# A fused attention, top-1 expert and tanh-MLP kernel: one-hot marks of twelve tiles and expert 0's weighing on ScalarE, float64 loads and conversions re-timed

## The chip, the cores and the metric

The kernel runs on one core of one Trainium2 chip. The metric is the device time of one execution, in microseconds (us); lower is better. Three runs of the kernel before took 1000.67, 1001.55 and 1002.6 us, median 1001.55 us. The program uses TensorE (PE, its weight load shown apart as PEld), VectorE (DVE), ScalarE (ACT), GpSimd (POOL) and the DMA queues, most of them issued by SyncE (SP).

## What is computed

Three stages follow each other. The reference, cut to what matters:

```python
# 1. linear attention, B, H, S, D = 4, 8, 768, 64
for t in range(S):
    state = gamma[None, :, None, None] * state + einsum('bhd,bhe->bhde', k[:, :, t], v[:, :, t])
    y[:, :, t] = scale * einsum('bhd,bhde->bhe', q[:, :, t], state)
# 2. top-1 mixture of experts, 3072 tokens, 512 features, 8 experts, 1024 hidden
logits = x @ w_gate;  e_idx = argmax(logits, axis=1);  gate_w = softmax(logits)[e_idx]
eom = sigmoid(x @ w_output_gate)
out[mask] = gate_w[mask, None] * eom[mask, e, None] * (maximum(x[mask] @ w1[e], 0) @ w2[e])
# 3. MLP, hidden 2048
h = x @ w_in;  out = (h - tanh(h)) @ w_out
```

The weights of the MLP come as float64 and everything else as float32. A float32 product is done as three matmuls of a high and a low part.

## The kernel before

**Tiles and stages.** The tokens are 24 tiles of 128 (`NT`, four sequences of six chunks). Stage one is the loop over `n` from 0 to 22 (with the tail behind it, L908 to L1075): in turn `n`, `attend(n)` computes the attention of tile n, `scores(n + 2)` the score matrix of the tile two ahead, and `rows(n)` turns tile n into token rows, stores them to `xtok` and gets the gate logits `lp`. Stage two runs the experts in steps of 128 hidden features (`mm1`, `mm2`), the largest-first order being found at run time; expert 0 is split into a head of 216 tokens (`PLACES[0]`) and a rest. Stage three runs 6 blocks of 512 tokens through 16 hidden slices (`mm3`, `act`, `mm4`).

**What sets the order.** Every engine works its own instructions in the order in which the program wrote them. The loop over n writes them by hand: operations of VectorE that may be late are kept in lists (`scales` for the gating, `convs` for the conversions) from which `fill` takes some at the end of each turn, up to `MOST` (2.6); those of ScalarE are taken by `pump`. SP works its DMAs in program order as well, and a DMA that waits holds all behind it.

**Turn n on TensorE** is: the state's part of the output (`qd`, `st`, L672), the state update (`up`, L680), the outputs (`o`, L690), the scores of tile n + 2 (`sc`, L631), and the transposes with the gate logits in their last columns (`tr`, L716). ScalarE copies the state (`st`, L684), then the outputs (`xT`, L699), which `tr` reads, then the rows (`xr`, L719), and issues their store. VectorE masks the scores (`pt`, L624) and sums the logits (`lp`, L723). GpSimd scales q and k (`qd`, `kd`).

**Gating.** The tiles are gated in groups of 8, 7 and 9 (`GROUPS`); the last group in three cuts. For a group: `onehot` finds each token's expert, `ranks` its rank among that expert's tokens, `scale` the gate value, and a **mark** per tile (L799) writes a 128 x 432 one-hot row of the rank, `ohr = (iota == rank)`. `slots` (`ip`, L859) multiplies the marks with the values into a table of slots. Behind group 1, `head` takes expert 0's first 216 slots from it and starts two gathers of token rows (`gx`); two turns later `weigh` multiplies them with the gate values (L391) and `half` transposes them (`xt`, L406), for `mm1(0)`.

**Conversions.** Each float64 piece (`m64`, two buffers) is loaded by `load_m` (L263) and converted by ten operations of `conv_m`: ScalarE takes the upper word (`keep`, L277), five VectorE operations build the float32 (L280, L283, L289, L293, L298), ScalarE rounds it to the high part (`keep` again, L305), VectorE subtracts (L310). L293 is the last reader of `m64`. Both parts are then stored (`dh`, `dl`, L312, L313). Five pieces are converted in stage one (numbers 27 to 31, pool `cva`, with two buffers each of `keep`, `ta` and `va`), the other 27 in stage two (pool `cv`, `keep` 3, `ta` 2, `va` 2); of these the last three are stored as well.

```python
if n > 0 and nload < NPA and len(m64) < 2 and n >= 2 * nload + 1:
    load_m(J0 + nload, cva_p)
...
if nconv < nload and n >= loaded_at[nconv] + 3:
    convs.append(piece(J0 + nconv, cva_p))
...
fill([scales, *convs], MOST - busy)
```

At n = 19 (`EARLIER`) the loop runs whatever is left of the conversions, since their pool is given to the experts.

Of the kernel before, what the change touches and what calls it, by code (L numbers as in the profile page):

```python
# [8 lines left out]
F32 = mybir.dt.float32  # L9
# [6 lines left out]
AF = mybir.ActivationFunctionType  # L16
ALU = mybir.AluOpType
# [6 lines left out]
P = 128  # L24
# [25 lines left out]
NV = 5 * E  # L50
GROUPS = (8, 7, 9)
TA = sum(GROUPS[:2])
MOST = 2.6
FAR = 1.0e6
PG = P + 2 * E
NPA = 5
# [77 lines left out]
def kernel(  # L134
# [30 lines left out]
    tri = cpool.tile([P, P], BF16, name="tri")  # L165
    ones = cpool.tile([P, P], BF16, name="ones")
    nc.vector.memset(ones, 1.0)
    rank = cpool.tile([P, NT], F32, name="rank")
    emax = cpool.tile([P, NT], F32, name="emax")
    gates = cpool.tile([P, NT], F32, name="gates")  # L170
# [85 lines left out]
            ops.pop(0)[1]()  # L256
            most -= 1

    m64, mcv, cv_bufs = {}, {}, {}

    def load_m(j, cv_p):
        t = cv_p.tile([P, DM], I64, tag="m64", name=f"m64_{j}", bufs=2)
# [3 lines left out]
    def conv_m(j, stage, cv_p):  # L266

        V = nc.vector
        f, cs = j // 2, slice((j % 2) * DM, (j % 2 + 1) * DM)

        def word(w):
            return m64[j].bitcast(U32).rearrange("p (n w) -> p n w", w=2)[:, :, w]

        def begin():
            t = {k: cv_p.tile([P, DM], U32, tag=k, name=f"{k}{j}", bufs=b) for k, b in cv_bufs[cv_p].items()}
            mcv[j] = t
            nc.scalar.activation(f32(t["keep"]), f32(word(1)), AF.Copy, scale=DOWN)  # L277

        def v0():
            V.tensor_scalar(mcv[j]["ta"], mcv[j]["keep"], 4, 1, op0=ALU.logical_shift_left, op1=ALU.logical_shift_right)  # L280

        def v1():
            V.scalar_tensor_tensor(  # L283
                out=mcv[j]["va"], in0=mcv[j]["keep"], scalar=0x80000000, in1=mcv[j]["ta"],
                op0=ALU.bitwise_and, op1=ALU.bitwise_or,
            )

        def v2():
            V.tensor_scalar(mcv[j]["ta"], mcv[j]["va"], 0xFF800000, None, op0=ALU.bitwise_and)  # L289

        def v3():
            sc = f32(mcv[j]["ta"])
            V.scalar_tensor_tensor(out=sc, in0=word(0), scalar=2.0 ** -52, in1=sc, op0=ALU.mult, op1=ALU.mult)  # L293
            m64.pop(j)

        def v4():
            vf = f32(mcv[j]["va"])
            V.tensor_tensor(out=vf, in0=vf, in1=f32(mcv[j]["ta"]), op=ALU.add)  # L298

        def high():  # L300
            if f < NRES:
                mcv[j]["hl"] = [x[:, cs] for x in wres[f]]
            else:
                mcv[j]["hl"] = [mcv[j][k].bitcast(F32R) for k in ("keep", "ta")]
            nc.scalar.activation(mcv[j]["hl"][0], f32(mcv[j]["va"]), AF.Copy)  # L305

        def rest():
            t = mcv.pop(j)
            hi, lo = t["hl"]
            V.tensor_tensor(out=lo, in0=f32(t["va"]), in1=f32(hi), op=ALU.subtract)  # L310
            if f >= NRES:
                stores.append(lambda: nc.sync.dma_start(wdram[f][0][:, cs], f32(hi)))  # L312
                stores.append(lambda: nc.sync.dma_start(wdram[f][1][:, cs], f32(lo)))  # L313

        return [
            [("A", begin)],
            [("V", v0), ("V", v1), ("V", v2)],
            [("V", v3), ("V", v4)],
            [("A", high)],
            [("V", rest)],  # L320
        ][stage]
# [64 lines left out]
    def weigh(p, c):  # L386
        rs = chunk(p, c)
        t = gxs[p, c][rs]
        rank_, c0, _ = PLACES[p]
        if p == 0:  # L390
            nc.vector.tensor_scalar(t, t, head_s[:, c:c + 1], None, op0=ALU.mult)  # L391
        elif p == 1:
            nc.vector.tensor_scalar(t, t, first_s[:, c0 + c, 0:1], None, op0=ALU.mult)
        else:
            nc.scalar.activation(t, t, AF.Copy, scale=sslot[rs, rank_, c:c + 1])
# [163 lines left out]
    with ExitStack() as actx:  # L559
# [221 lines left out]
            lg = t["lg"] if lg is None else lg  # L781
            nc.vector.tensor_tensor(out=t["z"], in0=t["oh"], in1=lg[:, :, E:2 * E], op=ALU.mult)

        def ranks(gi, n0, g0, g1, later=None):
            t = {k: v[:, g0:g1] for k, v in gst[gi].items() if k != "part"}
            G = g1 - g0
            oh = t["oh"]
            pre = bank("pt", f"pre{gi}_{g0}")[:, 0:G * E].rearrange("p (g e) -> p g e", e=E)
            nc.tensor.matmul(pre, ones, cnt.unsqueeze(1).to_broadcast([P, G, E]), start=True, stop=False)
            for g in range(G - 1):  # L790
                nc.tensor.matmul(
                    pre[:, g + 1:G], ones, oh[:, g].unsqueeze(1).to_broadcast([P, G - 1 - g, E]), start=False, stop=False
                )
            nc.tensor.matmul(pre, tri, oh, start=False, stop=True)
            nc.vector.tensor_tensor(out=t["rt"], in0=oh, in1=pre, op=ALU.mult)
            nc.vector.reduce_sum(out=rank[:, n0 + g0:n0 + g1], in_=t["rt"], axis=AX.X)
            for g in range(G):
                def mark(g=g):
                    nc.vector.tensor_scalar(  # L799
                        t["ohr"][:, g], iota, rank[:, n0 + g0 + g:n0 + g0 + g + 1], None, op0=ALU.is_equal  # L800
                    )

                if later is None:
                    mark()
                else:
                    later.append(("V", mark, 0.35))
            if G > 1:
                add = gp.tile([P, E], F32, tag="add", name=f"add{gi}_{g0}")
                nc.vector.reduce_sum(out=add, in_=oh.rearrange("p g e -> p e g"), axis=AX.X)
            else:  # L810
                add = oh[:, 0]
            nc.vector.tensor_tensor(out=cnt, in0=cnt, in1=add, op=ALU.add)
# [101 lines left out]
        nld = 4  # L914
        decay(2)
        J0 = 2 * NFM - NPA
        convs, scales, after = [], [], []
        due, now = {}, [0]
        nload, nconv, busy = 0, 0, 0.0
        loaded_at = []  # L920
        firsts = [sum(GROUPS[:i]) for i in range(len(GROUPS))]
        for n in range(NT - 1):
# [8 lines left out]
                flush()  # L931
                rooms()

            if n > 0 and nload < NPA and len(m64) < 2 and n >= 2 * nload + 1:
                load_m(J0 + nload, cva_p)
                loaded_at.append(n)
                nload += 1
# [3 lines left out]
            if n == TA or nld == NT:  # L941
                feed()
            flush()
            if nconv < nload and n >= loaded_at[nconv] + 3:
                convs.append(piece(J0 + nconv, cva_p))
                nconv += 1
            if n == 6:
                nc.gpsimd.tensor_copy(iota, ca[:, C_IOTA:C_IOTA + NS])
            if n > 0:
                attend(n)  # L950
            if n + 3 < NCH:
                decay(n + 3)
            pump(scales, False)
            for ops in convs:
                pump(ops, False)
# [7 lines left out]
                mm1(0)  # L963
            if n > 0:
                rows(n, gst[gi]["lp"][:, g])
            ready, after = after + due.pop(n, []), []
            for fn in ready:
                fn()

            q = n - (NT - 7)  # L970
            if 0 <= q < 3:
                conv_w(q, 0)
            if 1 <= q < 4:
                conv_w(q - 1, 1)
            if n == NT - 2:
                conv_w(3, 0)
                conv_w(3, 1)
            cuts = [0, G - 3, G - 1] if final else [0, G]
            if g + 1 in cuts[1:]:
                g0 = cuts[cuts.index(g + 1) - 1]  # L980
# [5 lines left out]
                if final and g + 1 == G - 1:  # L986
                    tail_a = a
                else:
                    hi = 2 * E if final else NV

                    def settle(a=a, hi=hi):
                        slots(a[0], a[2], a[3], 0, hi)
                        if a[0] == 1:
                            head()
                            for k in range(2):
                                due.setdefault(now[0] + 2, []).append(lambda k=k: weigh(0, k))
                            for kk in range(KD):
                                due.setdefault(now[0] + 2, []).append(lambda kk=kk: half(kk))

                    def place(a=a, hi=hi, settle=settle):  # L1000
                        ranks(*a, scales)
                        if a[0] == 1:
                            due.setdefault(now[0] + 1, []).append(close)
                        scales.append(("V", lambda: after.append(settle)))

                    after.append(place)
                    if not final:
                        scales += scale(gi, n0, g0, g + 1)
            fill([scales, *convs], MOST - busy)
            busy = 0.0  # L1010
            now[0] = n + 1
        run(scales)
        flush()
        gi, n0, G = len(GROUPS) - 1, firsts[-1], GROUPS[-1]
        for m in sorted(due):
            for fn in due[m]:
                fn()
        attend(NT - 1)
        if 0 not in hs:
            mm1(0)  # L1020
# [98 lines left out]
    for i in range(NFE, NSTEP + 1):  # L1119
# [25 lines left out]
        if i == CONV - 2:  # L1145
            whl2_p.release()
            cv_p = tc.alloc_tile_pool(name="cv", bufs=1, side="right", reuse_waits="tile")
            cv_bufs[cv_p] = dict(keep=3, ta=2, va=2)
            load_m(0, cv_p)
            load_m(1, cv_p)  # L1150
        for op in slot[1]:
# [307 lines left out]
```

## Time and profile before

| what | value |
|---|---|
| median of three runs | 1001.55 us (1000.67 to 1002.6) |
| the profiled execution: its own time | 1006.25 us |
| its span (first to last instruction) | 1004.5 us |
| PE busy | 971.4 us (97%) |
| PEld busy | 841.9 us (84%) |
| DVE busy | 759.4 us (76%) |
| ACT busy | 602.5 us (60%) |
| POOL busy | 375.1 us (37%) |
| mean granted TensorE clock | 0.981 of full speed |

All times below are counted from the start of the span. An engine's busy share is an average over the stages: stage one ends at about 146 us, where the rest of expert 0 begins, the experts at about 459 us, the MLP at the end. A wait in the views is named by the tile that waits, the line that wrote the instruction, and the tile or transfer that released it; where the engine named had long been done, a transfer released it.

### The profile page before, as it was taken

To read this page: it belongs to the slowest core of one execution; us is meant where nothing else is said; L and a number is where in the kernel's file an instruction comes from. 1 tells how busy PE (TensorE), PEld (TensorE's weight loads), DVE (VectorE), ACT (ScalarE), POOL (GpSimd) and SP (SyncE) were. 2 spreads that over 40 slices of the span, in tenths; PEclk is the share of its full clock that TensorE was granted. 3 is DMA by queue.
4 is the path that set the end of the run, shared out by engine and by line. 5 is a ranking of instruction groups with operands and counts; after the bars stand their busy time and mean duration, and the time that the engine had idled before them with its cause. 6 is when DMAs were issued, how large, how long until landed. Compare 5 with 4: busy or idle time off the path is not lost. (4 is left out here: it accounts for less than half of the span.)

```text
span 1004.5 us, 16476 instructions
## 1 busy us (share of the span) xinstructions
PE 971.4 (97%) x5942; PEld 841.9 (84%) x5942; DVE 759.4 (76%) x1189; ACT 602.5 (60%) x1090; POOL 375.1 (37%) x327
## 2 busy tenths in 40 slices
PE   8889889999999999999999999999999999999995
PEld 6778779999999999998888888888888888888884
DVE  2688667788889899866977777777777777777772
ACT  3434333655556565646866776766676767677662
POOL 4553512344354344232432433252343325323322
PEclk9999789999999999999999999999999999999998
DMA  9989624577577677666000100010010001000001
GB/s 333 343 348 368 217 85 146 158 230 218 179 233 221 187 238 222 190 213 219 22 11 11 42 21 22 11 53 11 12 42 22 22 1 54 10 1 21 22 1 45
DMA packets 43579, 120.70 MB, mean 120 GB/s; under 512 B 9334, under 2 KB 14710, under 8 KB 40546
## 3 DMA queue, kind: packets, MB, share of 16 engines
q1 hardware_dynamic: 34450, 99.31, 30.2%
q0 software_dynamic: 4864, 12.91, 4.2%
q10 hardware_dynamic: 4176, 7.36, 2.0%
q8 instruction: 48, 0.79, 0.3%
q14 instruction: 41, 0.34, 0.1%
HBM read 95.99 MB, written 23.57 MB: 119 GB/s over the span
## 5 line engine op out<-in xcount | busy, mean ns | idle before, releaser
L1207 POOL TENSOR_TENSOR gl<-g,gh 128x512 fp32r<-128x512 f32 x96 | 124.0, 1292 | 343.4 <-ACT gh L1206 328.3
L241 POOL TENSOR_TENSOR wl<-wr,wh 128x512 fp32r<-128x512 f32 x64 | 90.2, 1409 | 179.8 <-ACT wh L239 176.2
L1200 DVE COPY_PREDICATED g<-big,td 128x512 f32<-128x512 int32 x96 | 145.2, 1513 | 9.9
L1225 PE MATMUL mh<-x2h,ml 128*128 128x512 f32 x384 | 152.7, 398 | 0.0
L1225 PE MATMUL mh<-x2l,mh 128*128 128x512 f32 x384 | 152.4, 397 | 0.0
L1225 PE MATMUL mh<-x2h,mh 128*128 128x512 f32 x384 | 151.9, 396 | 0.0
L1239 PE MATMUL ma<-ml,gh 128*128 128x512 f32 x384 | 151.3, 394 | 0.0
L1239 PE MATMUL ma<-mh,gh 128*128 128x512 f32 x384 | 151.1, 393 | 0.0
L1239 PE MATMUL ma<-mh,gl 128*128 128x512 f32 x384 | 149.3, 389 | 0.0
L1190 DVE SCALAR_TENSOR_TENSOR g<-s,mh 128x512 f32<-128x512 f32 x96 | 65.9, 686 | 102.1 <-ACT s L1188 86.1
L1186 ACT ACTIVATE u<-mh 128x512 f32<-128x512 f32 x96 | 57.4, 598 | 128.8 <-PE mh L1225 124.7
L239 ACT ACTIVATE wh<-wr 128x512 fp32r<-128x512 f32 x136 | 83.5, 626 | 81.6 <-PE ya L453 75.5
L429 PE MATMUL ph<-xh,wh 128*128 128x216 f32 (+7 forms) x288 | 98.2, 341 | 0.0
L453 PE MATMUL ya<-lo,wh 128*128 128x216 f32 (+7 forms) x288 | 95.6, 332 | 1.8 <-DVE lo L433 1.8
L453 PE MATMUL ya<-hi,wh 128*128 128x216 f32 (+7 forms) x288 | 95.8, 333 | 0.0
L429 PE MATMUL ph<-xl,wh 128*128 128x216 f32 (+7 forms) x288 | 95.3, 331 | 0.4 <-DVE xl L411 0.4
L429 PE MATMUL ph<-xh,wl 128*128 128x216 f32 (+7 forms) x288 | 95.3, 331 | 0.3 <-POOL wl L241 0.3
L453 PE MATMUL ya<-hi,wl 128*128 128x216 f32 (+7 forms) x288 | 95.5, 332 | 0.0
L1225 PEld LDWEIGHTS mh<-x2h,ml 128*128 128x128 f32 x384 | 72.3, 188 | 17.6
L1225 PEld LDWEIGHTS mh<-x2h,mh 128*128 128x128 f32 x384 | 72.5, 189 | 17.1
L1239 PEld LDWEIGHTS ma<-mh,gh 128*128 128x128 f32 x384 | 72.0, 188 | 17.5
L1225 PEld LDWEIGHTS mh<-x2l,mh 128*128 128x128 f32 x384 | 72.0, 188 | 17.1
(183 smaller groups left out, 2021.6 us busy)
## 6 DMA issues: line engine op xcount, KB each, us to landing
wr<-in_w SPq DMA_DIRECT2D x68, 512.0 KB, 4.5
ld<-in_qkv SPq DMA_DIRECT2D x23, 1024.0 KB, 9.7
m<-in_w SPq DMA_DIRECT2D x32, 512.0 KB, 6.8
xtok<-xr ACTq DMA_DIRECT2D x24, 256.0 KB, 5.8
x2r<-x2c SPq DMA_DIRECT2D x24, 256.0 KB, 2.7
dh<-keep SPq DMA_DIRECT2D x8, 256.0 KB, 8.0
dl<-ta SPq DMA_DIRECT2D x8, 256.0 KB
mh<-dh SPq DMA_DIRECT2D x4, 512.0 KB, 7.8
```

What stands on the lines that cost most here:

```text
L239: nc.scalar.activation(hi, t[:, cs], AF.Copy)
L241: eng.tensor_tensor(out=lo, in0=t[:, cs], in1=f32(hi), op=ALU.subtract)
L429: nc.tensor.matmul(ph, a[:, cs], b[:, kk, 0:ns], start=(k == 0), stop=(k == 3 * KD - 1))
L453: nc.tensor.matmul(accs[p][dk], a[:, cs], b, start=(k == 0 and j == 0 and (p > 0 or dk % 2 == 0)), stop=(k == NFE - 1 and j == 2), skip_gr ...
L1186: nc.scalar.activation(u, h, AF.Square)
L1190: nc.vector.scalar_tensor_tensor(out=g, in0=s1, scalar=PB1, in1=h, op0=ALU.add, op1=ALU.mult)
L1200: nc.vector.copy_predicated(g, big.bitcast(I32), td)
L1207: nc.gpsimd.tensor_tensor(out=lo, in0=g, in1=f32(hi), op=ALU.subtract)
L1225: nc.tensor.matmul(h, a[:, cs], c, start=(k == 0), stop=(k == 3 * KD - 1))
L1239: nc.tensor.matmul(macc[b][t], a[:, cs], c[:, DM:2 * DM], start=(f == 0 and j == 0), stop=(f == NFM - 1 and j == 2))
```

## The change

Four things are edited in stage one and one number in stage two. (1) The marks of group 0 (all 8) and of group 1's last 4 tiles are written by ScalarE, as `Square(rank - iota)` and then `Relu(1 - 2 x)` in place, mostly one tile a turn, instead of by one VectorE comparison. (2) The weighing of expert 0's head is a ScalarE copy with a scale, at the start of its turn instead of behind the rows. (3) Float64 pieces are loaded two turns behind the turn in which their buffer's last reader was written, and converted two turns later instead of three; until turn 14, `fill` takes conversions ahead of gating. The first two weight conversions of the experts are written one turn later. (4) Pool `cv` has three `ta` buffers. (`due` now comes ahead of `after`, and the last weight conversion of the loop comes behind `fill`.)

```diff
+MARKED = (0, 3)
-    m64, mcv, cv_bufs = {}, {}, {}
+    m64, mcv, cv_bufs, freed, now = {}, {}, {}, {}, [0]
@@ conv_m, v3
             m64.pop(j)
+            freed[j] = now[0]
@@ weigh
         if p == 0:
-            nc.vector.tensor_scalar(t, t, head_s[:, c:c + 1], None, op0=ALU.mult)
+            nc.scalar.activation(t, t, AF.Copy, scale=head_s[:, c:c + 1])
@@ ranks
+                def mark_act(g=g):
+
+                    col = rank[:, n0 + g0 + g:n0 + g0 + g + 1]
+                    nc.scalar.activation(t["ohr"][:, g], iota, AF.Square, scale=-1.0, bias=col)
+                    nc.scalar.activation(t["ohr"][:, g], t["ohr"][:, g], AF.Relu, scale=-2.0, bias=one)
+
                 if later is None:
                     mark()
+                elif on_act is not None and g >= MARKED[gi]:
+                    on_act.append(mark_act)
                 else:
                     later.append(("V", mark, 0.35))
@@ the loop
-            if n > 0 and nload < NPA and len(m64) < 2 and n >= 2 * nload + 1:
+            if 0 < n and nload < NPA and (nload < 2 or n >= freed.get(J0 + nload - 2, NT) + 2):
                 load_m(J0 + nload, cva_p)
...
-            if nconv < nload and n >= loaded_at[nconv] + 3:
+            if nconv < nload and n >= loaded_at[nconv] + (3 if nconv < 2 else 2):
                 convs.append(piece(J0 + nconv, cva_p))
...
+            for fn in begun.pop(n, []):
+                fn()
             if n > 0:
                 attend(n)
...
+            mark_one(n)
             pump(scales, False)
...
-            ready, after = after + due.pop(n, []), []
+            ready, after = due.pop(n, []) + after, []
...
-            q = n - (NT - 7)
+            q = n - (NT - 6)
...
-                                due.setdefault(now[0] + 2, []).append(lambda k=k: weigh(0, k))
+                                begun.setdefault(now[0] + 2, []).append(lambda k=k: weigh(0, k))
...
-            fill([scales, *convs], MOST - busy)
+            if n >= TA:
+                mark_one(n)
+            fill([scales, *convs] if n >= TA - 1 else [*convs, scales], MOST - busy)
+            if n == NT - 2:
+                conv_w(3, 0)
+                conv_w(3, 1)
@@ stage two
-            cv_bufs[cv_p] = dict(keep=3, ta=2, va=2)
+            cv_bufs[cv_p] = dict(keep=3, ta=3, va=2)
```

How the order of the engines moves is shown at three places. **VectorE, turns 17 and 18** (`ohr` a mark, `pt` the masked scores of the tile two ahead, `wl` a weight's low part, `va` and `ta` the last piece's conversion). Before:

```order
L842 CAST part_822<-s_819 128x7
L846 TENSOR_TENSOR ohv_810<-oh_809,part_822 128x7x8
L799 TENSOR_SCALAR ohr_812<-iota,rank 128x432 x5
L624 TENSOR_TENSOR pt_1589<-sc_0_1590,ca 128x512
L624 TENSOR_TENSOR pt_1589<-sc_1_1591,ca 128x512
L723 TENSOR_REDUCE lp_1354<-tr_0_1609 128x16
L723 TENSOR_REDUCE lp_1354<-tr_1_1614 128x16
L241 TENSOR_TENSOR wl_0_1625<-wr_1316,wh_0_1624 128x512
L799 TENSOR_SCALAR ohr_812<-iota,rank 128x432 x2
L298 TENSOR_TENSOR va_1352<-va_1352,ta_1351 128x512
L310 TENSOR_TENSOR ta_1351<-va_1352,keep_1350 128x512
```

Now:

```order
L854 CAST part_826<-s_823 128x7
L858 TENSOR_TENSOR ohv_814<-oh_813,part_826 128x7x8
L803 TENSOR_SCALAR ohr_816<-iota,rank 128x432 x3
L628 TENSOR_TENSOR pt_1604<-sc_0_1605,ca 128x512
L628 TENSOR_TENSOR pt_1604<-sc_1_1606,ca 128x512
L727 TENSOR_REDUCE lp_1337<-tr_0_1624 128x16
L727 TENSOR_REDUCE lp_1337<-tr_1_1629 128x16
L628 TENSOR_TENSOR pt_1692<-sc_0_1693,ca 128x512
```

Four of the seven marks, the weight's low part and the end of the last conversion no longer stand between the masked scores of turn 17 and those of turn 19; the conversion now ends in turn 13.

**ScalarE, turns 9 and 10** (`m_29`, `m_30` are pieces 29 and 30; `tau`, `ex`, `th` belong to the gating of group 0). Before:

```order
L699 ACTIVATE xT_905<-o_879 128x512
L825 ACTIVATE tau_264<-dl_261 128x64
L826 ACTIVATE ex_271<-zs_269 128x8
L827 ACTIVATE th_270<-zs_269 128x8
L719 ACTIVATE xr_926<-tr_0_927 128x256
L719 ACTIVATE xr_926<-tr_1_932 128x256
L724 DMA xtok<-xr_926 128x512
L684 ACTIVATE st<-up 128x256
L699 ACTIVATE xT_980<-o_954 128x512
L277 ACTIVATE keep_982<-m_30_695 128x512
```

Now:

```order
L703 ACTIVATE xT_906<-o_880 128x512
L810 ACTIVATE ohr_270<-iota,rank 128x432
L811 ACTIVATE ohr_270<-ohr_270,one 128x432
L309 ACTIVATE keep_802<-va_804 128x512
L280 ACTIVATE keep_911<-m_30_697 128x512
L723 ACTIVATE xr_931<-tr_0_932 128x256
L723 ACTIVATE xr_931<-tr_1_937 128x256
L728 DMA xtok<-xr_931 128x512
L688 ACTIVATE st<-up 128x256
L703 ACTIVATE xT_980<-o_954 128x512
```

A mark of two instructions and the high part of piece 29 (in turn 12 before) now stand between `xT` and `xr` of turn 9, and piece 30 begins there instead of in turn 10.

**SP, from the stores of piece 28 on.** Before:

```order
L312 DMA dh_102<-keep_655 128x512
L313 DMA dl_103<-ta_656 128x512
L603 DMA ld_952<-in_qkv 128x2048
L603 DMA ld_1024<-in_qkv 128x2048
L263 DMA m_31_1082<-in_w 128x512
L603 DMA ld_1084<-in_qkv 128x2048
```

Now:

```order
L316 DMA dh_104<-keep_598 128x512
L317 DMA dl_105<-ta_599 128x512
L607 DMA ld_878<-in_qkv 128x2048
L266 DMA m_31_948<-in_w 128x512
L607 DMA ld_950<-in_qkv 128x2048
```

Piece 31, which before stood behind the loads of tiles 15 and 16, stands behind that of tile 14; the stores of piece 28 stand ahead of tile 14's load instead of behind it.

## Rows read from the trace of the kernel before

**Rows 1.** Windows of the trace: busy us (instructions), clock, DMA share, GB/s.
```profile
50.00:100.00 50.00, 46.99 (x730) 40.90 (x729) 42.08 (x127) 19.85 (x50) 23.07 (x32) 0.97 0.93 358
100.00:125.00 25.00, 20.74 (x240) 18.16 (x243) 17.17 (x45) 8.76 (x20) 12.79 (x15) 0.73 0.67 225
...
200.00:225.00 25.00, 25.00 (x135) 23.95 (x135) 22.05 (x31) 14.17 (x27) 11.77 (x9) 1.00 0.76 228
109.10:122.70 13.60, 11.62 (x102) 10.50 (x104) 6.94 (x20) 3.93 (x9) 3.83 (x5) 0.50 0.62 192
132.95:136.36 3.41, 3.39 (x40) 2.75 (x41) 1.84 (x6) 1.06 (x2) 0.00 (x0) 0.50 0.02 5
```
**Rows 2.** What TensorE waited for, 100 to 160 us: total, times, longest.
```profile
PE sc L631 <- DVE pt L624: 3.0, 1, 3.0
PE xt L406 <- DVE gx L391: 2.8, 1, 2.8
PE pre L791 <- DVE oh L759: 2.0, 2, 1.6
```
**Rows 3.** Timeline of TensorE: start, duration, idle before in brackets.
```profile
77.07 1.73 PE L859 MATMUL ip<-ohv,ohr 128*108 128x40 bf16 x32
...
86.27 1.25 PE L716 MATMUL tr<-turn_rhs,xT 128*128 128x144 f32 x8
...
90.62 1.25 PE L716 MATMUL tr<-turn_rhs,xT 128*128 128x144 f32 x8
...
103.50 1.25 PE L716 MATMUL tr<-turn_rhs,xT 128*128 128x144 f32 x8
...
123.59 1.25 PE L716 MATMUL tr<-turn_rhs,xT 128*128 128x144 f32 x8
...
138.81 1.16 PE L716 MATMUL tr<-turn_rhs,xT 128*128 128x144 f32 x8
```
**Rows 4.** Timeline of VectorE: marks of both groups, the end of piece 31.
```profile
70.52 1.29 DVE L799 TENSOR_SCALAR ohr<-iota,rank 128x432 bf16<-128x432 f16 x5
...
105.58 3.62 DVE L799 TENSOR_SCALAR ohr<-iota,rank 128x432 bf16<-128x432 f16 x5
...
111.59 0.68 DVE L298 TENSOR_TENSOR va<-va,ta 128x512 f32<-128x512 f32 x1
```
**Rows 5.** Timeline of ScalarE: a wait of turn 19, a calm turn, a wait of turn 10.
```profile
112.31 0.63 ACT L305 ACTIVATE keep<-va 128x512 fp32r<-128x512 f32 x1 [5.59 <-DVE va L298]
...
85.30 0.60 ACT L699 ACTIVATE xT<-o 128x512 f32<-128x512 f32 x1
87.45 0.66 ACT L719 ACTIVATE xr<-tr 128x256 f32<-128x256 f32 x2 [1.55 <-DMA xtok<-xr]
...
68.42 0.66 ACT L277 ACTIVATE keep<-m 128x512 f32<-128x512 f32 x1 [4.79 <-issue]
```
**Rows 6.** ScalarE by line and form: instructions with a per-partition bias or scale.
```profile
L1188 ACT ACTIVATE s<-u,cb 128x512 f32<-128x512 f32 x96 | 69.6, 725 | 3.1
...
L395 ACT ACTIVATE gx<-gx,sslot 108x512 f32<-108x512 f32 x22 | 14.8, 709 | 0.0
```
**Rows 7.** The second head gather: its issue on GpSimd, and DMA issues to landing.
```profile
121.60 1.01 POOL L380 DMA_INDIRECT gx<-xtok,head_idx  x1 [0.31 <-DMA wr<-in_w]
...
gx<-xtok,head_idx POOLq DMA_INDIRECT x2, 4.7
```
**Rows 8.** Timeline of VectorE, turn 22: the weight's low part.
```profile
141.97 1.35 DVE L241 TENSOR_TENSOR wl<-wr,wh 128x512 fp32r<-128x512 f32 x1 [0.59 <-ACT wh L239]
```
**Rows 9.** Stage two: VectorE before piece 26, and TensorE behind it.
```profile
434.86 0.43 DVE L280 TENSOR_SCALAR ta<-keep 128x512 uint32<-128x512 uint32 x1 [3.27 <-ACT wh L239]
...
437.93 0.43 PE L453 MATMUL ya<-lo,wh 128*128 128x368 f32 x1 [1.76 <-DVE lo L433]
```
**Rows 10.** Timeline of SP: piece 31's load, and the loads around it.
```profile
59.19 3.51 SPq L603 DMA_DIRECT2D ld<-in_qkv  x2
75.37 0.33 SPq L263 DMA_DIRECT2D m<-in_w  x1
```

More of the change, by code (lines that the diff above doesn't have):

```diff
@@ L167 @@
     nc.vector.memset(ones, 1.0)
+    one = cpool.tile([P, 1], F32, name="one")
+    nc.vector.memset(one, 1.0)
     rank = cpool.tile([P, NT], F32, name="rank")
@@ L782, in chosen, with ranks @@
             nc.vector.tensor_tensor(out=t["z"], in0=t["oh"], in1=lg[:, :, E:2 * E], op=ALU.mult)
-        def ranks(gi, n0, g0, g1, later=None):
+        def ranks(gi, n0, g0, g1, later=None, on_act=None):
             t = {k: v[:, g0:g1] for k, v in gst[gi].items() if k != "part"}
@@ L916, with mark_one @@
         J0 = 2 * NFM - NPA
-        convs, scales, after = [], [], []
-        due, now = {}, [0]
+        convs, scales, after, acts, marked = [], [], [], [], [NT]
+        def mark_one(n):
+            if acts and n > marked[0]:
+                acts.pop(0)()
+                if len(acts) == 1:
+                    acts.pop(0)()
+        due, begun = {}, {}
         nload, nconv, busy = 0, 0, 0.0
@@ L974 @@
                 conv_w(q - 1, 1)
-            if n == NT - 2:
-                conv_w(3, 0)
-                conv_w(3, 1)
             cuts = [0, G - 3, G - 1] if final else [0, G]
@@ L995, in settle, with place, settled @@
                             for k in range(2):
-                                due.setdefault(now[0] + 2, []).append(lambda k=k: weigh(0, k))
+                                begun.setdefault(now[0] + 2, []).append(lambda k=k: weigh(0, k))
                             for kk in range(KD):
                                 due.setdefault(now[0] + 2, []).append(lambda kk=kk: half(kk))
-                    def place(a=a, hi=hi, settle=settle):
-                        ranks(*a, scales)
+                    def place(a=a, hi=hi, settle=settle, final=final):
+                        todo = [1 if final else 2]
+                        def settled(todo=todo):
+                            todo[0] -= 1
+                            if not todo[0]:
+                                after.append(settle)
+                        ranks(*a, scales, None if final else acts)
+                        marked[0] = now[0]
                         if a[0] == 1:
                             due.setdefault(now[0] + 1, []).append(close)
-                        scales.append(("V", lambda: after.append(settle)))
+                        scales.append(("V", settled))
+                        if not final:
+                            acts.append(settled)
                     after.append(place)
@@ L1014 @@
         gi, n0, G = len(GROUPS) - 1, firsts[-1], GROUPS[-1]
-        for m in sorted(due):
-            for fn in due[m]:
-                fn()
+        for fns in (begun, due):
+            for m in sorted(fns):
+                for fn in fns[m]:
+                    fn()
         attend(NT - 1)
```

## The prediction, made blind

> **What bounds the kernel now.** I read the windows first. In the experts TensorE is busy without a break at full clock ([rows 1], 200 to 225 us), and the waits of TensorE behind 160 us add up to little, so stages two and three can only be moved forward as a whole by what stage one gives back. Stage one is another matter: from 50 to 100 us TensorE works 47.0 of 50 us with the DMA engines 0.93 busy, but from 100 to 125 us only 20.7 of 25, at a mean clock of 0.73 and with the DMA at 0.67 [rows 1]. There it waits for other engines and runs slowly; memory is not what stops it.
>
> Next the timeline of TensorE [rows 3]. A calm turn, from one `tr` to the next, takes 90.62 - 86.27 = 4.35 us. From turn 18 (103.50) to turn 20 (123.59) two turns took 20.09 us, from turn 20 to turn 22 (138.81) 15.22 us. The waits [rows 2] name three places: the scores for VectorE's masking, 3.0 us; the transposes of expert 0's head for the weighing on VectorE, 2.8 us; the last ranks for the one-hot of the experts, 1.6 of 2.0 us. None of the larger ones is for a load. Each long wait has a price behind it: after the first one the clock is granted at 0.50 (1.2 instead of 2.4 GHz) for 13.60 us, after the second for 3.41 us [rows 1].
>
> Then why VectorE was late. Five marks of group 1 took 3.62 us at 105.58, the same five of group 0 1.29 us at 70.52, that is 0.72 and 0.26 us each [rows 4]. They stood ahead of the masking of turn 18; the end of piece 31 came behind them at 111.59 [rows 4], and ScalarE, which needs it, idled 5.59 us until 112.31 with everything of turn 19 queued behind [rows 5].
>
> **The change, part by part.** All of it is reckoned against the profiled execution (span 1004.5 us, its own time 1006.25); the median of the runs, 1001.55, lies 4.70 below that time, and I take the sum off the median.
>
> *Marks and conversions away from turns 17 to 19.* The order shows four of seven marks, a weight part and the end of piece 31 gone from VectorE there. Two turns should then cost 2 x 4.35 plus the slot matmuls of group 1. Those 28 I price by the 32 of group 0, 1.73 us at full clock [rows 3]: 28/32 x 1.73 = 1.5. So 10.2 in place of 20.09: **-9.9 us**. Ends: 0, if another engine holds the same turns up (below), and -9.9, since a calm turn is the floor.
>
> *The slots of group 0* move from turn 12 to turn 17, the same 1.73 us on TensorE: 0. Their readers are settled only behind group 1's slots, so nobody waits for them.
>
> *The 12 marks on ScalarE.* The nearest instruction is a Square with a per-partition bias on 128 x 512, 0.725 us [rows 6]; at 432 of 512 columns I estimate 0.61, two of them 1.2 us a mark (ends 1.2 and 2 x 0.725 = 1.45), 12 marks 14.6 to 17.4 us. What hides them: in the calm turn 14, ScalarE ends `xT` at 85.90 and starts `xr` at 87.45, 1.55 us of idling [rows 5], and the marks stand mostly there, one a turn. I cost them at 0. In turns 9 and 12 a conversion's 0.66 us stands beside the mark and overruns the gap by 0.3; `st` of the next turn has that much to spare.
>
> Here a rule of the Trainium skill speaks against the change: ScalarE: Activation LUTs, section Rules for kernel authors, puts `relu` and `mul` on VectorE, not on ScalarE. The trace agrees about the price of one mark (0.26 to 0.72 against 1.2 us). If every microsecond of both engines counted, as the rule has it, 12 marks would cost 14.6 and give back 3.1 to 8.7, a loss of 6 to 11 us; by the gap of 1.55 us it is 0. This rule is the first rival.
>
> *The weighing on ScalarE and turns 20 to 22.* Two calm turns, plus about 1.5 us for the eight transposes of the head, a rank product and `mm1(0)` being longer than a score (my estimate from the calm turn's pieces), are 10.2 instead of 15.22 us: 5.0 to win. But the weighing now stands ahead of `st` and `xT` of turn 21, and the gathers are issued in turn 19. Counted from `tr` of turn 19: it ends at 1.25, the slots at 2.75; before, the second gather was issued at 121.60, 5.8 us behind the start of the slots, which ran at half clock, so I take 4.4; issued at 5.65, landed 4.7 later [rows 7] at 10.35, weighed in 0.71 [rows 6], `st` and `xT` to 11.95. TensorE wants that `xT` at 5.85 + 4.35 = 10.2. So a new wait of 1.75 us, and I add one window at half clock behind it, 3.41/2 = 1.7 [rows 1]. Left: **-1.55 us**; ends -5.0 and 0.
>
> *The low part of weight 3* (1.35 us, [rows 8]) stood ahead of the one-hot for which TensorE waited 1.6 us; now it comes behind `fill`: **-1.35 us**; ends -1.6 and 0.
>
> *Loads and conversions up to turn 12.* SP had issued its last load by 62.70 and then nothing until piece 31 at 75.37 [rows 10], 12.7 us of blocking for VectorE's L293 of piece 29. That blocking goes, but TensorE shows no wait for a load behind it, so 0 for itself. ScalarE idled 4.79 us at the start of piece 30 in turn 10, for nothing the profile names [rows 5]; the buffer it writes is one of two `keep`, still being stored for piece 28. Now piece 30 begins a turn earlier, and that store stands one load earlier: about the same wait, 0. Ends: -4.8 (the wait goes) and +4.8 (piece 31, whose buffer is that of piece 29, stored two turns before, waits as long). Piece 28's load now stands ahead of tile 7's; it was ahead of tile 8's before, and tile 8's comes as it did: 0.
>
> *Third `ta` buffer in stage two.* VectorE idled 3.27 us before piece 26; the named `wh` had long been done, and piece 24's low part was being stored from the same buffer. TensorE waited 1.76 us behind it [rows 9]. With a third buffer the store has a whole piece longer: **-1.76 us**; ends -1.76 and 0.
>
> Sum: 9.9 + 1.55 + 1.35 + 1.76 = 14.6 us off 1001.55: **987.0 us**.
>
> **Rivals.**
>
> 1. *ScalarE becomes the chain (slower).* Place: turns 9 to 18, mark between `xT` and `xr`. Then `xr`, its store, `st` of the next turn and the `qd` product behind it are late. For it: ScalarE works in order, the second instruction of a mark reads what the first wrote, and in turns 17 and 18 two marks are written. Against it: 1.55 us free [rows 5]. It decides where a mark costs more than 1.55 us, or 0.9 beside a conversion. If the whole mark enters the chain, 12 x 1.45 = 17.4 us eat the 14.6, and one more window at half clock adds 1.7: 1001.55 + 4.5 = 1006. Chance 0.10.
> 2. *Waits for `keep`.* The stores of the pieces hold ScalarE once more, at piece 31 in turn 12: 4.8 us, and a window at half clock, 1.7. For it: the 4.79 us of turn 10 and a DMA at 0.93; against it: the mark ahead gives the store 1.2 us more. 987.0 + 6.5 = 993.5. Chance 0.16.
> 3. *The clock stays low.* Some shorter wait in turns 18 to 20 brings the same 13.60 us at 0.50 instead of one window of 3.41: (13.60 - 3.41)/2 = 5.1 more, 992. For it: a wait of 2.8 us was enough for a window. Chance 0.10.
> 4. *The change doesn't do what it says.* The slow marks are slow because GpSimd works beside them, and three remain on VectorE; if masking stays late, or the head's gather holds turn 21 as long as the old waits did, only the last two terms are left, less what the new wait costs: 999 to 1001. Chance 0.05.
>
> **How the numbers follow.** The forecast has 0.59. About 0.2% (2 us) is what a measurement of this kernel can tell from no change. The forecast and rivals 2 and 3 are faster by more, 0.85; rival 4 counts as the same, 0.05; rival 1 as slower, 0.10. The range: down, the new wait and its window do not come (-3.45) and half of the early wait goes (-2.4): 981. Up, rival 2 with half of rival 3 and the `ta` term missing: 993.5 + 2.5 + 1 = 997. Rival 1 and most of rival 4 stay outside.
>
> **What would show it.** Right: `tr` of turn 20 follows that of turn 18 by about 10 us at full clock; no idling of ScalarE for L302 (the old L298) at turn 19; marks of about 0.6 us an instruction behind `xT`; an `xT` wait of TensorE of 1 to 3 us in turn 21; stage one ending near 133 us instead of 146; no 1.76 us gap in the last expert. Wrong: calm turns longer than 4.35 us between turns 9 and 17 (rival 1); ScalarE idle at `keep` in turns 9 and 12 and `tr` of turn 12 later than before (rival 2); a half clock over more than 3.4 us in turns 18 to 20 (rival 3); the same scores wait for `pt` (rival 4).

## The result and the profile after

| kernel | median | runs |
|---|---|---|
| before | 1001.32 us | 4 (1000.67 to 1002.6) |
| changed | 992.77 us | 4 (992.64 to 994.12) |

The changed kernel takes 0.9916 of the time of before (95% interval 0.9899 to 0.9933), 8.5 us less, where 14.6 us were forecast. Its profiled execution took 992.64 us, near its median (span 990.9, clock 0.992), while the profiled execution of before lay 4.9 us above that kernel's median. The two traces are therefore not subtracted here. The kernel before was profiled once more (first experiment, 1002.03 us, span 1000.3), and the comparison by steps uses that trace.

TensorE of the changed kernel, timeline (start, duration, idle before in brackets), cut to `tr`, the slots, the head's transposes and the first matmul of `mm1(1)`:

```profile
101.81 1.25 PE L720 MATMUL tr<-turn_rhs,xT 128*128 128x144 f32 x8
106.55 1.25 PE L720 MATMUL tr<-turn_rhs,xT 128*128 128x144 f32 x8 [0.32 <-ACT xT L703]
107.64 1.53 PE L871 MATMUL ip<-ohv,ohr 128*108 128x40 bf16 x28
112.28 1.25 PE L720 MATMUL tr<-turn_rhs,xT 128*128 128x144 f32 x8
118.19 1.25 PE L720 MATMUL tr<-turn_rhs,xT 128*128 128x144 f32 x8 [1.48 <-ACT xT L703]
119.27 0.54 PE L410 MATMUL xt<-cb,gx 108*128 108x108 f32 x4
122.71 0.98 PE L410 MATMUL xt<-cb,gx 108*128 108x108 f32 x4 [2.90 <-DVE lp L727]
...
128.32 1.16 PE L720 MATMUL tr<-turn_rhs,xT 128*128 128x144 f32 x8
...
134.32 0.34 PE L433 MATMUL ph<-xh,wh 128*128 128x216 f32 x1
```

The `tr` are those of turns 18 to 22. Turns 18 to 20 now take 112.28 - 101.81 = 10.47 us, and the 28 slot matmuls 1.53 us; before they took 20.09 [rows 3]. Turns 20 to 22 take 16.04 us, more than the 15.22 of before [rows 3]. The scores' wait for masking, 3.0 us, and the transposes' wait for the weighing, 2.8 us [rows 2], are gone; a wait for `xT` (1.48) and one of the head's second half for `lp` (2.90) are there instead.

Windows of the changed kernel: the stretches of [rows 1], then the only two stretches at half clock ahead of the last 10 us of the span (us, busy us and instructions of the engines, clock, DMA share, GB/s):

```profile
50.00:100.00 50.00, 48.31 (x766) 41.73 (x764) 44.79 (x135) 32.85 (x74) 26.48 (x36) 1.00 0.98 381
100.00:125.00 25.00, 20.31 (x317) 17.55 (x313) 15.64 (x41) 14.79 (x30) 13.25 (x15) 0.95 0.57 188
200.00:225.00 25.00, 25.00 (x138) 23.91 (x137) 21.68 (x29) 14.92 (x28) 7.36 (x7) 1.00 0.57 176
```

```profile
40.70:44.11 3.41, 3.41 (x29) 3.13 (x30) 2.18 (x5) 0.82 (x3) 3.36 (x7) 0.50 1.02 429
122.62:126.03 3.41, 3.32 (x47) 2.92 (x49) 2.32 (x9) 1.05 (x2) 0.00 (x0) 0.50 0.03 10
```

From 100 to 125 us the clock is 0.95 in place of 0.73, and the 13.60 us at half clock [rows 1] are gone. Each of the two stretches that are left stands behind a long wait: the second behind the 2.90 us above, the first behind the wait for tile 7's load:

```profile
39.57 1.16 PE L635 MATMUL sc<-ld 64*128 64x128 f32 x16 [2.94 <-DMA ld<-in_qkv]
```

ScalarE from 60 to 110 us by lines (count, busy us, mean ns, idle before):

```profile
L811 ACT ACTIVATE ohr<-ohr,one 128x432 bf16<-128x432 bf16 x12 | 7.9, 655 | 0.4
L810 ACT ACTIVATE ohr<-iota,rank 128x432 bf16<-128x432 f16 x11 | 7.1, 647 | 0.4 <-ACT xr L723 0.4
L280 ACT ACTIVATE keep<-m 128x512 f32<-128x512 f32 x2 | 1.3, 666 | 0.0
```

A mark is 0.65 + 0.65 us, and `keep` of pieces 30 and 31 waited for nothing; before, piece 30 stood behind 4.79 us of idling [rows 5].

### The profile page after: what moved, and what is told of

Its sections match the earlier page's. It is cut to its first block, busy times and chain, and to the rows that moved or that the text cites. A ratio compares the mean times of both kernels' runs of the same rounds, so it can differ in the third digit from the quotient of the medians.

```text
span 990.9 us, 16486 instructions
## 1 busy us (share of the span) xinstructions
PE 963.9 (97%) x5942; PEld 832.5 (84%) x5942; DVE 754.4 (76%) x1176; ACT 618.5 (62%) x1116; POOL 375.4 (38%) x327
## 5 line engine op out<-in xcount | busy, mean ns | idle before, releaser
L1237 DVE COPY_PREDICATED g<-big,td 128x512 f32<-128x512 int32 x96 | 143.1, 1491 | 12.1 <-DVE td L1236 2.3
L1276 PE MATMUL ma<-mh,gl 128*128 128x512 f32 x384 | 151.5, 395 | 0.0
L1276 PEld LDWEIGHTS ma<-ml,gh 128*128 128x128 f32 x384 | 72.0, 188 | 17.5
```

The lines of the kernel that those rows point to most:

```text
L1237: nc.vector.copy_predicated(g, big.bitcast(I32), td)
L1276: nc.tensor.matmul(macc[b][t], a[:, cs], c[:, DM:2 * DM], start=(f == 0 and j == 0), stop=(f == NFM - 1 and j == 2))
```

## The experiments

Each kernel was run beside the kernel before on the same chip. Over the three groups before ran 57 times, 1000.4 to 1009.1 us, with medians 1002.6, 1002.88 and 1002.12. "mm1(1)" is the start of the first matmul after stage one, from the trace.

| kernel | median us (runs) | ratio to before, 95% | mm1(1) |
|---|---|---|---|
| before_again | 1002.25 (12) | 1.0004 (0.9982 to 1.0026) | 144.48 |
| b_ta3 | 1000.55 (12) | 0.9973 (0.9953 to 0.9992) | 144.66 |
| b_marks | 1001.97 (12) | 0.9981 (0.9961 to 1.0001) | 139.49 |
| a_marksV | 994.46 (6) | 0.9905 (0.9872 to 0.9939) | 137.52 |
| after_again | 994.94 (5) | 0.9919 (0.9904 to 0.9935) | 136.63 |
| b_one | 1004.68 (12) | 1.0020 (1.0007 to 1.0033) | 142.73 |
| a_oneA1 | 993.52 (5) | 0.9903 (0.9886 to 0.9919) | 134.90 |
| a_weighBehind | 994.85 (6) | 0.9918 (0.9901 to 0.9936) | 135.55 |
| b_loads | 996.49 (6) | 0.9941 (0.9919 to 0.9963) | 137.51 |
| a_oldloads | 995.21 (6) | 0.9927 (0.9906 to 0.9948) | 136.67 |
| best1 | 989.84 (4) | 0.9872 (0.9847 to 0.9896) | 133.34 |
| best2 | 991.32 (4) | 0.9884 (0.9862 to 0.9907) | 134.77 |

### Was the profile of before a typical one?

No edit (before_again).

> The kernel before, unchanged. Theory: the profiled execution of before was 4.7 us slower than its median because of the long stretch at half clock between turns 18 and 20 (13.6 us at 0.50, 6.8 us of work lost); a typical execution does not have it: own time 1000.7 to 1002.6 us, mean clock 0.985 to 0.990, turns 18 to 20 in 13.5 to 16 us in place of 20.09. Rival: every execution has it, as the first profile (span near 1004.5, clock 0.981, 20 us for the two turns), and the change gave back 5 us elsewhere.

TensorE of this second profile of before, timeline, and its windows at half clock:

```profile
101.98 1.25 PE L716 MATMUL tr<-turn_rhs,xT 128*128 128x144 f32 x8
...
112.26 2.29 PE L716 MATMUL tr<-turn_rhs,xT 128*128 128x144 f32 x8 [1.23 <-ACT xT L699]
...
122.75 1.25 PE L716 MATMUL tr<-turn_rhs,xT 128*128 128x144 f32 x8
...
137.45 0.79 PE L716 MATMUL tr<-turn_rhs,xT 128*128 128x144 f32 x5
```

```profile
67.96:71.37 3.41, 3.25 (x26) 2.97 (x28) 3.38 (x11) 0.88 (x3) 1.48 (x2) 0.50 0.63 253
108.92:122.57 13.65, 12.38 (x114) 11.35 (x114) 5.63 (x17) 4.28 (x9) 4.05 (x4) 0.50 0.69 231
132.81:136.22 3.41, 3.41 (x46) 2.81 (x34) 2.44 (x8) 0.90 (x3) 0.00 (x0) 0.50 0.00 0
```

The theory falls: this execution of 1002.03 us has the long stretch too, and turns 18 to 20 took 20.77 us. The traces of b_ta3 and b_one, whose stage one is that of before, have it as well: 13.65 us at half clock in each. This second profile is shorter than the first elsewhere: 1.5 us up to turn 18, and 2.6 us from `mm1(1)` to the MLP, where the first profile has two more stretches at half clock. So the large term of the prediction was rightly sized also for a usual execution, and what is missing went somewhere else.

### The third buffer alone

```diff
-            cv_bufs[cv_p] = dict(keep=3, ta=2, va=2)
+            cv_bufs[cv_p] = dict(keep=3, ta=3, va=2)
```

> Before with the third ta buffer in stage two alone. Theory (the term of the prediction): the 1.76 us gap of TensorE in the last expert goes, nothing else changes: 1.0 to 2.0 us faster, 999.5 us. Rival: VectorE was held by something else there, and the gap stays: 0, within 0.5 us.

1.7 us faster by the medians; from `mm1(1)` to the first `mh` it took 307.28 us in place of 309.37, and TensorE waits for nothing there. The theory stands.

### Marks and loads, one without the other

b_marks is before with edit 1 alone; b_loads is before with edit 3 alone (without its later weight parts, the tile `one` out of the constants and unread); both have `due` ahead of `after`, as the changed kernel has. a_marksV and a_oldloads are the changed kernel with one of them undone:

```diff
@@ a_marksV
-MARKED = (0, 3)
+MARKED = (8, 7)
@@ a_oldloads
-            if 0 < n and nload < NPA and (nload < 2 or n >= freed.get(J0 + nload - 2, NT) + 2):
+            if n > 0 and nload < NPA and len(m64) < 2 and n >= 2 * nload + 1:
...
-            if nconv < nload and n >= loaded_at[nconv] + (3 if nconv < 2 else 2):
+            if nconv < nload and n >= loaded_at[nconv] + 3:
...
-            fill([scales, *convs] if n >= TA - 1 else [*convs, scales], MOST - busy)
+            fill([scales, *convs], MOST - busy)
```

> Before with the twelve marks on ScalarE alone (loads, conversions, weighing, weight parts and ta as before). Theory: the marks were what made the masking of turn 18 late; most of the long stall between turns 18 and 20 goes: 3 to 6 us faster than before. Rival A: the last piece's conversion, still beside turn 19, holds ScalarE and the turns all the same: within 1.5 us of before. Rival B (the first rival of the prediction): ScalarE becomes the chain, 1 us or more slower than before.

> The changed kernel with all its marks on VectorE again (the earlier loads and conversions, the weighing on ScalarE and ta 3 stay). Theory: the marks stand before the masking of turns 17 and 18 again, the scores wait 2 us or more there: 3 to 6 us slower than the changed kernel (996 to 999). Rival A: with the conversions out of the way VectorE has room for the marks: within 1.5 us of 992.8. Rival B: marks on ScalarE cost more than they give: faster than 992.8 by 1 us or more.

> Before with the edit of the loads and conversions alone (pieces loaded two turns behind their free buffer, converted two turns later, conversions ahead of gating until turn 14; all marks and the weighing on VectorE, weight parts and ta as before, the MLP's tiles where they lay). Theory: moving the conversions out of turns 17 to 19 is enough by itself to end VectorE's lateness there; turns 18 to 20 take 9 to 12 us in place of 20.8, and the whole is 4 to 7 us faster than before (996 to 998.5). Rival: the marks that stay ahead of the masking hold the scores all the same: within 1.5 us of before.

> The changed kernel with the old condition for loads and conversions, and gating ahead of conversions again (marks and weighing on ScalarE, ta 3 and the tile of ones stay). Theory: the last piece is converted beside turns 17 to 19 again and ScalarE waits for it, as with the marks alone in before, where turns 18 to 20 took 16.1 us: 2 to 5 us slower than the changed kernel (996.5 to 999.5); tile 7 comes as before, without its wait of 2.9 us. Rival: with the marks on ScalarE the loads don't matter: within 1 us of the changed kernel.

From `tr` of turn 16 to that of turn 20 the traces give: before_again 30.1 us, b_marks 26.3, b_loads 22.8, a_marksV 23.1, a_oldloads 20.6, changed 19.7. (The 32 slot matmuls of group 0, 1.73 us, stand in these turns in all but before_again; the 28 of group 1, about 1.5 us, stand in them in all but b_loads and a_marksV, which have them behind turn 20.) The waits of TensorE from 90 to 125 us in b_marks, then in b_loads:

```profile
PE tr L720 <- ACT xT L703: 2.4, 1, 2.4
PE sc L635 <- DVE pt L628: 0.3, 1, 0.3
```

```profile
PE sc L635 <- DVE pt L628: 1.9, 2, 1.6
PE ip L871 <- DVE lp L727: 1.4, 1, 1.4
```

With the marks moved the masking is in time, but the last conversion and the high parts of the weights, both on ScalarE ahead of `xT`, still hold it 2.4 us. With the conversions moved, the marks still hold the masking, but less. Each edit alone brings stage one's end forward, by 5.0 and 7.0 us against before_again; the whole change brings it forward by 8 to 10. The two mend the same lateness, and their gains don't add up.

In whole times b_loads did what its theory said: 5.6 us, with turns 18 to 20 in 11.93 us. b_marks took the time of its rival A: its interval includes no difference. With the loads moved, the marks on ScalarE or on VectorE make no difference that these runs can tell (a_marksV against after_again, 994.46 and 994.94), and with the marks moved the loads make none (a_oldloads, 995.21): both theories missed there. b_marks also showed something that no theory had: 5.0 us sooner into stage two, but only 0.3 us by the medians and 2.4 by the spans. Part of this is the execution that was profiled, whose 999.69 us lie 2.3 us under its kernel's median.

One part of the change was in no theory and in no run alone: the first three weights (not two, as said above) are converted a turn later. In turns 16 to 20 b_marks and a_oldloads differ in that alone, and they take 26.3 and 20.6 us. So with the marks moved, the later weight parts are worth 5.7 us there, by one execution of each kernel. With the loads moved instead they bring nothing (b_loads 22.8, a_marksV 23.1).

### Where b_marks lost it: the MLP

Behind the first `mh` matmul nothing in stage three is edited. Yet it is longer in the changed kernel, in b_marks and in a_marksV than in before_again and b_ta3. What the three share is the small tile `one`, which sits among the constants and so moves the tiles behind it by 32 bytes, among them `mh`, `ml` of the first twelve hidden slices and `x2h`, `x2l` (x2h0 from byte 120640 to 120672). Two kernels test it: before with the tile, unread, and the changed kernel with the tile in a pool of stage one.

```diff
@@ b_one
     nc.vector.memset(ones, 1.0)
+    one = cpool.tile([P, 1], F32, name="one")
+    nc.vector.memset(one, 1.0)
@@ a_oneA1
-    one = cpool.tile([P, 1], F32, name="one")
...
         a1p = actx.enter_context(tc.tile_pool(name="attn1", bufs=1))
+        one = a1p.tile([P, 1], F32, name="one")
+        nc.vector.memset(one, 1.0)
```

> The changed kernel, unchanged, beside the next three. Expected by all theories: median 992 to 994.5 us; stage three (first mh matmul to the end of the span) 548.5 us, where before took 546.4.

> Before plus the constant tile of ones (128 x 1 float32, set once and read by nobody), which moves every tile of the left side behind it by 32 bytes, the MLP's weights mh and ml and its inputs x2h and x2l among them. Theory: the 2.0 to 2.7 us that stage three lost in the changed kernel come from these addresses alone: 2.0 to 2.7 us slower than before, stage three 548.4 to 549.1 us, stages one and two as before. Rival: the loss comes from the order or from the chip's state in that execution: 0 within 0.7 us, stage three 546.4.

> The changed kernel with its tile of ones taken from stage one's pool instead of the pool of constants, so that the MLP's tiles lie where they lay before. Theory: stage three falls from 548.5 to 546.4 us, the whole by 2.0 to 2.7 us, to 990.3. Rival (not the addresses): same as the changed kernel within 0.7 us.

Two lines of each trace by source line (count, duration min/median/max in ns, first and last start), one of `mm3` and one of `mm4`: before_again, b_one, the changed kernel, a_oneA1.

```profile
L1225 PE MATMUL mh<-x2h,mh x384: 392/396/398, 453.8 to 974.3; 128*128 128x512 f32 x192
L1239 PE MATMUL ma<-mh,gl x384: 387/389/389, 468.3 to 988.4; 128*128 128x512 f32 x192
```

```profile
L1227 PE MATMUL mh<-x2h,mh x384: 392/397/403, 452.4 to 975.5; 128*128 128x512 f32 x192
L1241 PE MATMUL ma<-mh,gl x384: 388/395/397, 466.9 to 989.7; 128*128 128x512 f32 x192
```

```profile
L1262 PE MATMUL mh<-x2h,mh x384: 392/397/402, 442.4 to 965.5; 128*128 128x512 f32 x192
L1276 PE MATMUL ma<-mh,gl x384: 388/395/397, 456.9 to 979.7; 128*128 128x512 f32 x192
```

```profile
L1262 PE MATMUL mh<-x2h,mh x384: 392/396/398, 442.6 to 963.1; 128*128 128x512 f32 x192
L1276 PE MATMUL ma<-mh,gl x384: 387/389/390, 457.1 to 977.2; 128*128 128x512 f32 x192
```

From the first to the last `mh` line it takes 520.5 us where the tiles lie as before, and 523.1 with the tile among the constants, in both kernels. All fourteen traces fall on one of the two sides: seven take 520.5 us (no such tile, or the tile in stage one's pool) and seven 523.1 (the tile among the constants), and in each of them TensorE is busy without a gap at full clock from 460 to 960 us. So the cause is shown: 2.6 us of the MLP come from where 128 x 4 bytes are put. Most of it lies in one group of matmuls, `ma<-mh,gl`, of which the median takes 395 ns in place of 389; added up from start to start, this group takes 89.1 us in place of 86.7. Which tile's address does it, and how, is not shown: the hidden slices 12 to 15, whose weights did not move, lose in this group too.

The whole times carry less: by the medians it is 1.8 us for b_one (ratio above 1 beyond its interval) and 1.4 for a_oneA1, with overlapping intervals. after_again lay 2.2 us above the first median of the same kernel, and 0.4 above what all theories expected of it.

### Turns 20 to 22

a_weighBehind moves the loop over `begun` behind `attend(n)`. best1 has that, the tile as in a_oneA1, and two weight parts later; best2 also swaps the two loading statements.

```diff
@@ best1
-            if 1 <= q < 4:
-                conv_w(q - 1, 1)
+            if q == 1:
+                conv_w(0, 1)
...
             fill([scales, *convs] if n >= TA - 1 else [*convs, scales], MOST - busy)
+            if n == NT - 3:
+                conv_w(1, 1)
+                conv_w(2, 1)
```

> The changed kernel with the weighing of expert 0's head on ScalarE behind st and xT of turn 21 instead of ahead of them. Theory: the 1.48 us wait of TensorE for xT in turn 21 goes, but the second half of the head's transposes still waits for the sums of the logits (lp), which stand on VectorE behind a weight part of 3.23 us and a one-hot chain, and that wait grows by as much: 0 to 1 us faster. Rival: the xT wait is what counts, and its 1.5 us are won whole, with the clock staying up behind it, 1.5 to 3.2 us faster.

> The changed kernel with the MLP's tiles in their old places, the weighing behind xT, and the low parts of weights 1 and 2 (VectorE) behind turn 21's work instead of ahead of the one-hot of turn 20. Theory: the sums of logits of turn 21 are then written by 119.5 and the transposes' wait of 2.90 us and the stretch at half clock behind it (1.7 us lost) go: turns 20 to 22 take 11 to 13 us in place of 16.0, the whole 986 to 989.5. Rival: the one-hot chain alone (2.7 us on VectorE) still holds the sums, or the split of the head comes late in its place: turns 20 to 22 stay over 14.5 us, and the time is that of the tiles' places alone, 990 to 993.5.

> The kernel before this one, with each tile's load issued ahead of a float64 piece's load of the same turn. Theory: the scores' wait of 2.94 us for tile 7 (turn 5) falls by about one piece's transfer, 1.4 us or more, and the half clock behind it goes: 1 to 3.5 us faster than the kernel before this one. Rival: the DMA engines are the bound there (0.93 and more busy), the wait moves to the next tile or to the conversions: within 0.7 us.

The head's second transposes in a_weighBehind:

```profile
123.92 0.98 PE L410 MATMUL xt<-cb,gx 108*128 108x108 f32 x4 [4.44 <-DVE lp L727]
```

The `xT` wait of 1.48 us is gone, and the `lp` wait grew by as much, from 2.90 to 4.44 us; turns 20 to 22 stay at 16.03. The theory holds. What makes `lp` late is seen on VectorE of the changed kernel, and on GpSimd beside it:

```profile
110.11 0.69 DVE L244 TENSOR_TENSOR wl<-wr,wh 128x512 fp32r<-128x512 f32 x1
...
113.98 0.19 DVE L727 TENSOR_REDUCE lp<-tr 128x16 f32<-128x32 f32 x1 [0.21 <-ACT xr L723]
115.54 3.23 DVE L244 TENSOR_TENSOR wl<-wr,wh 128x512 fp32r<-128x512 f32 x1 [1.36 <-ACT wh L242]
118.69 0.78 DVE L748 TENSOR_TENSOR lg<-lp 128x96 f32<-128x96 f32 x1
...
120.16 0.21 DVE L754 SCALAR_TENSOR_TENSOR t<-dl,ca 128x48 f32<-128x48 f32 x1
...
121.27 1.28 DVE L628 TENSOR_TENSOR pt<-sc,ca 128x512 f32<-128x512 f32 x2
122.47 0.28 DVE L727 TENSOR_REDUCE lp<-tr 128x16 f32<-128x32 f32 x2
```

```profile
114.44 1.42 POOL L645 TENSOR_TENSOR qd<-ld,qt 128x256 f32<-128x256 f32 x2
115.81 1.17 POOL L651 TENSOR_TENSOR kd<-ld,ca 128x256 f32<-128x256 f32 x2
116.95 1.25 POOL L244 TENSOR_TENSOR wl<-wr,wh 128x512 fp32r<-128x512 f32 x1
118.17 1.88 POOL L645 TENSOR_TENSOR qd<-ld,qt 128x256 f32<-128x256 f32 x2
```

The weight part, 0.69 us at 110.11, took 3.23 at 115.54. best1 moved it away, and its rival came true in a form that it had not named. VectorE of best1, then GpSimd:

```profile
115.23 0.39 DVE L751 TENSOR_TENSOR dl<-lg,m 128x48 f32<-128x48 f32 x1
115.65 3.03 DVE L754 SCALAR_TENSOR_TENSOR t<-dl,ca 128x48 f32<-128x48 f32 x1
118.72 0.20 DVE L762 TENSOR_REDUCE emax<-t 128x6 f32<-128x48 f32 x1
```

```profile
114.78 1.46 POOL L645 TENSOR_TENSOR qd<-ld,qt 128x256 f32<-128x256 f32 x2
116.20 1.18 POOL L651 TENSOR_TENSOR kd<-ld,ca 128x256 f32<-128x256 f32 x2
117.35 1.26 POOL L242 TENSOR_TENSOR wl<-wr,wh 128x512 fp32r<-128x512 f32 x1
```

An instruction of 48 elements, 0.21 us in the changed kernel, now takes 3.03 us and ends as GpSimd's `wl` does. So it is not the weight part that is slow: in both traces the VectorE instruction that starts at about 115.6 us, beside GpSimd's unbroken run, is held until 118.7. The other traces of kernels with the later weight parts and the marks on ScalarE have the same hold, of 3.24 or 3.25 us on the weight part and of 3.03 in best2. The Trainium skill, SBUF — State Buffer, section SBUF: two separate sides, calls the ports that VectorE and GpSimd share an exclusive lock, held for one whole instruction. The trace agrees in that VectorE is stopped and not slowed (0.69 and 0.21 us both grew, by 2.5 and 2.8 us), but the stop covers several GpSimd instructions and not one. That GpSimd is the cause is read from these times and not shown: moving GpSimd's part was not tried, and in the first profile of before a GpSimd run from 102.32 to 110.24 us held no VectorE instruction for so long.

best1 is still the fastest kernel of the study, 0.9872 of before; its interval lies below those of the changed kernel's two measurements. Its 989.84 us lie between the two ranges, above the 989.5 of its theory and under the 990 of its rival; its turns 20 to 22 take 14.71 us, which is the rival's. Its profile keeps a stretch at half clock behind the 2.98 us wait for `lp`. In best2 the wait of 2.5 us for a tile's load became two of 0.5 and 1.1 us, as its rival said of the next tile, but the whole is not faster: 991.32, 1.5 us above best1 where the rival allowed 0.7, with overlapping intervals.

## Why the prediction was right in its mechanism and 5.8 us off

The forecast by steps, against the second profile of before and the profile of the changed kernel, in us:

| step | before_again | changed | difference | predicted |
|---|---|---|---|---|
| start to `tr` of turn 18 | 101.98 | 101.81 | -0.2 | 0 |
| turns 18 to 20 | 20.77 | 10.47 | -10.3 | -9.9 |
| turns 20 to 22 | 14.70 | 16.04 | +1.3 | -1.55 |
| `tr` of turn 22 to `mm1(1)` | 7.03 | 6.00 | -1.0 | -1.35 |
| `mm1(1)` to the first `mh` | 309.37 | 308.11 | -1.3 | -1.76 |
| first `mh` to the end | 546.4 | 548.4 | +2.0 | 0 |
| span | 1000.3 | 990.9 | -9.4 | -14.6 |

Of the 5.2 us between the last two columns, 2.9 belong to turns 20 to 22 and 2.0 to stage three.

*Marks and conversions away from turns 17 to 19* held: 10.47 us against 10.2 in the forecast, at full clock. The experiments add that its parts overlap. The loads alone gave turns 18 to 20 in 11.93 us and 5.6 us of the whole; the marks alone gave 16.12 us there and no whole time that the runs can tell; and the later weight parts, which the prediction names only in passing, are worth 5.7 us beside the marks.

*The weighing and turns 20 to 22* is the step that failed in size. "So a new wait of 1.75 us, and I add one window at half clock behind it" came out as 1.48 us, and behind it stood a second wait of 2.90 us that the prediction did not have, with the half clock behind that one: +1.3 us in place of -1.55. Not seen was that the second half of the head's transposes needs the bank that VectorE's `lp` of the same turn must first read, and that VectorE would be 3 us late there. The row that bore on it was in the trace of before, where a 128 x 512 weight part took 1.35 us [rows 8], about twice the 0.69 of others, beside a weight part of GpSimd (141.50 to 142.77); I took it as work, not as a hold.

*Stage three* had no term at all: "stages two and three can only be moved forward as a whole". It cost 2.0 us by the table and 2.6 us from the first `mh` matmul to the last, through an edit of one 128 x 1 tile that I had not listed.

*The low part of weight 3* gave about what was forecast. *The third buffer* gave 2.1 us alone, and 1.3 here, where a wait of 0.7 us for a weight part of GpSimd is new. *Loads up to turn 12*: the 4.79 us wait for `keep` went, and with it TensorE's wait of 2.7 us for `xT` behind it; but tile 7 came 2.94 us late behind piece 28, with a stretch at half clock. The prediction saw that piece 28's load now stands ahead of tile 7's and answered only for tile 8 ("tile 8's comes as it did: 0"); tile 7's lateness had no term. The two errors cancel to -0.2, which is luck. *Marks at 0* held: 1.3 us each, inside the estimate of 1.2 to 1.45.

The rivals: 992.77 lies beside the times of rivals 2 and 3, but neither happened. ScalarE no longer waits for a store of `keep` (its waits there are for VectorE's `va`, 2.15 us at most), and turns 18 to 20 have no stretch at half clock. Rival 1 didn't come: calm turns such as 74.45 to 78.81 stay at 4.36 us, and in the longer turn from 59.71 to 65.80 ScalarE was done with its mark at 60.58 and then waited 2.15 us for `va`. The rule that the Trainium skill gives, ScalarE: Activation LUTs, Rules for kernel authors, is right about the price of a mark (1.3 against 0.26 to 0.72 us [rows 4]), but that price fell into ScalarE's idle time; b_marks reached stage two 5.0 us sooner in spite of it.

Not settled: what makes executions of one kernel differ by up to 8.6 us, beyond that the second profile of before has fewer stretches at half clock than the first. The table by steps sets one execution of each kernel against the other; in the second trace of the changed kernel (after_again) turns 18 to 20 again take 10.47 us, but turns 20 to 22 take 17.3.

## What to carry to other kernels

Cost a change by every address it moves, not only by its instructions: a new constant tile belongs into the pool of the stage that uses it, and a stage that no edit touches should be timed from its first to its last matmul. The gains of two edits that mend the same lateness don't add up; run each alone before keeping both, and also the small edits made in passing. Before predicting that a wait goes, look up who else must read the same bank, and whether that engine may be late itself, as VectorE was here beside a long run of GpSimd.

## What the runs showed of the hardware

- The 2242 matmuls that the traces have from the first `mh` matmul of stage three to the last, at full clock and without a gap, take 520.5 or 523.1 us, depending on a shift by 32 bytes of tiles that they read, in seven traces each.
- A VectorE instruction of 0.21 us took 3.03 us beside unbroken GpSimd work, 14 times its usual time, and one of 0.69 us took 3.23 in the same place.
- In the changed kernel the two stretches at half clock stand behind single waits: behind waits of 2.94 and 2.90 us TensorE was granted 0.50 for 3.41 us each. With the stalls of turns 18 to 20 gone, the mean clock from 100 to 125 us went from 0.73 to 0.95.
